# An index load moved to SyncE's queue, and VectorE's work around the first expert in another order

## Chip, core and metric

The kernel runs on one core of a Trainium2 chip. The metric is the device time of one execution in microseconds, the median of several runs. TensorE (PE in the profile) multiplies, VectorE (DVE) and ScalarE (ACT) work element by element, GpSimd (POOL) issues the indirect transfers, and SyncE (SP) issues the other transfers from one queue in program order.

## What is computed

```python
attn_out = _attn_ref(q, k, v, lam)          # decayed linear attention, (4, 8, 768, 64)
x = attn_out.transpose(0, 2, 1, 3).reshape(3072, 512)
logits = x @ w_gate                          # 8 experts
e_idx = np.argmax(logits, axis=1)
gate_w = probs[np.arange(N), e_idx]          # softmax of the logits
eom = 1.0 / (1.0 + np.exp(-(x @ w_output_gate)))
for e in range(E):
    mask = e_idx == e
    h = np.maximum(x[mask] @ w1[e], 0.0)     # 512 -> 1024
    ye = h @ w2[e]                           # 1024 -> 512
    out[mask] = gate_w[mask, None] * eom[mask, e, None] * ye
```

Every token goes to one of eight experts, so the tokens must be sorted by expert before the second half.

## The kernel before

**First half.** The attention runs over 24 tiles of 128 tokens (6 chunks by 4 batches). Each finished tile is transposed by VectorE (`stage_d2`) and written to a table of rows in memory, `x_d`. After every four tiles the router ranks their tokens (`route_choose`, `route_place`), and `place_scatter` lets GpSimd scatter one record a token (its output row, its scale, its row of `x_d`) into a table `tab_d`, which is ordered by expert and place.

**Second half.** The experts are worked off from the fullest to the emptiest. For each, the index rows are read back out of `tab_d` (`load_rows`), turned into row numbers on VectorE (`row_index`, which writes `rows`), the tokens' rows are fetched from `x_d` by GpSimd (`gather`), transposed (`x_turn`), and split into a high and a low float32r part (`x_split`). The weights come in pieces of 1 MB (`load_piece` on SyncE, into one of three `raw` buffers) and are split the same way: ScalarE makes the high part (`split_hi`, L132, `whi`), VectorE the low part (`split_lo2`, L146, `wlo`). Each product is three matmuls: high by high, low by high, high by low (L85, L86, L87).

**The first expert.** It starts before the last four tiles are routed. Its 448 rows come in three parts. The first 192 are gathered early. The middle rows, below place `LATE` = 352, are read once the first five groups of tiles are scattered: `load_rows(0, 1, 3, nc.gpsimd)` reads their index from GpSimd's own queue. The last 96 are picked from the last four tiles on TensorE (`take_late`, the tile `chosen`) and split by `split_late`. `units` is the list of TensorE's work on the first 192 rows: eight columns `fc` of the up product (tiles `ph`, 12 matmuls each), then two blocks of the down product (`pyr`, 24 matmuls each; the first block reads pieces 2 and 3, that is `w2`). `fill(n)` takes n units from it, and `settle()` makes the activations of those that are done: `hhi` on ScalarE (L1009) and `hlo` on VectorE (L1010). After the down blocks TensorE goes on with the up product for rows 192 to 447.

**What sets the order.** Inside `manual_schedule` every engine runs its instructions in the order in which the code writes them. Semaphores hold an instruction until its inputs are there, and everything behind it on that engine or queue then waits too. The stretch that the change touches stands between the last attention tile and the loop over the experts:

```python
place_scatter(B)                       # the last tiles' records
settle()
for h in range(2):
    split_lo2(1, h)
...
row_index(0, 1)
gather(0, 6, 11, LAST * P)
stage_d2(LAST + 1)
stage_d2(n - 1, 2)
split_late()
sort_rest(counts)
...
    fill(8)
    split_lo2(2, h)
    settle()
```

Of the kernel before, what the change touches and what calls it, by code (L numbers as in the profile page):

```python
# [23 lines left out]
def kernel(  # L24
# [96 lines left out]
    def split_hi(i, j):  # L121
        if i >= len(pieces):
            return
        if pieces[i] not in wparts:
            wparts[pieces[i]] = (
                wpool.tile([P, 4, 512], F32R, tag="whi", bufs=4, name=f"whi_{i}"),
                wpool.tile([P, 4, 512], F32R, tag="wlo", bufs=4, name=f"wlo_{i}"),
            )
        src, hi = raws[i][:, j, :], wparts[pieces[i]][0][:, j, :]
        if turned_out(i):  # L130
            src, hi = by_quarter(src), by_part(hi)
        nc.scalar.copy(out=hi, in_=src)  # L132
# [163 lines left out]
    def blank_rows():  # L296
        norow = wpool.tile([P, E * EB * 3], I32, tag="raw", bufs=3, name="norow")
        nc.gpsimd.memset(norow, NOROW)
        nc.sync.dma_start(tab_d.rearrange("(p r) t -> p (r t)", p=P), norow)


    later = []
# [220 lines left out]
    def stage_d2(n, count=1):  # L523
        if count == 1:
            xn = slot(f"xn_{n}")
        else:
            xn = pool.tile([P, 8 * P], F32, tag="wide", bufs=4, name=f"xn_{n}")
        for i in range(count):

            src = live[n + i]["xT"].rearrange("p (g b r) -> p b g r", g=NPAIR, b=4)  # L530
            dst = xn[:, i * DM : (i + 1) * DM].rearrange("p (b g c) -> p b g c", b=4, g=NPAIR)
            nc.vector.transpose(dst, src)
            weave()
        nc.sync.dma_start(
            x_d[n * P : (n + count) * P, :].rearrange("(i p) m -> p i m", p=P),
            xn[:, 0 : count * DM].rearrange("p (i m) -> p i m", m=DM),
        )
# [133 lines left out]

    pending = []

    def place_scatter(count):
        for _ in range(min(count, len(pending))):
            idx, rec = pending.pop(0)
            scatter(
                "table",
                nc.gpsimd.indirect_dma_start(  # L679
                    out=tab_d,  # L680
                    out_offset=bass.IndirectOffsetOnAxis(ap=idx, axis=0),
                    in_=rec,
                    in_offset=None,
                    bounds_check=P * E * EB - 1,
                    oob_is_err=False,
                ),
            )

    def scatter(group, ins):
        inst = getattr(ins, "ins", ins)  # L690
        tc.declare_no_dep(inst, group=group, reason="these scatters write different rows")
        tc.add_to_no_dep_group(group, inst)
# [135 lines left out]
    def load_rows(p, j0=0, j1=None, eng=nc.sync):  # L828
        if p >= E:
            return  # L830
        n = (KT[p] if j1 is None else j1) - j0
        t = const.tile([32, 4, n, 3], I32, name=f"index_{p}_{j0}")
        src = tab_v[bass.ds(expert[p], 1)][:, :, j0 : j0 + n, :]
        eng.dma_start(t, src.rearrange("e (b r) j t -> (e r) b (j t)", b=4))
        idxs[(p, j0)] = (t, n)

    def load_outs(p, j0=0, j1=None):
        if p >= E:
# [25 lines left out]
    def row_index(p, j0=0):  # L864
        if p >= E:
            return
        t, n = idxs[(p, j0)]
        gf = const.tile([32, 4, n], F32, name=f"rowf_{p}_{j0}")
        nc.vector.scalar_tensor_tensor(
            out=gf, in0=t[:, :, :, 2], scalar=float(4 * NT), in1=t[:, :, :, 2], op0=ALU.is_lt, op1=ALU.mult  # L870
        )
        gi = const.tile([P, 4, n], I32, name=f"rows_{p}_{j0}")
        for qq in range(4):
            nc.vector.tensor_scalar(
                out=gi[32 * qq : 32 * qq + 32], in0=gf, scalar1=float(P * qq), scalar2=None, op0=ALU.add
            )
        for j in range(n):
            for bb in range(4):
                gis[(p, 4 * (j0 + j) + bb)] = gi[:, bb, j : j + 1]
# [326 lines left out]
    def settle():  # L1206
        while acts:
            acts.pop(0)()
# [8 lines left out]
    with tc.manual_schedule():  # L1217
# [126 lines left out]
        for f in held[6:]:  # L1344
            f()
        place_scatter(B)
        load_rows(0, 1, 3, nc.gpsimd)
        stage_c(n - 1)
        for g in range(NPAIR):
            x_hi(0, g, 0)  # L1350
# [30 lines left out]
        fill(4)  # L1381
        take_late(LAST)
        at_once(place[4:])
        place_scatter(B)
        settle()
        for h in range(2):
            split_lo2(1, h)
        for j in range(4):
            split_hi(2, j)
        row_index(0, 1)  # L1390
        gather(0, 6, 11, LAST * P)
        stage_d2(LAST + 1)
        stage_d2(n - 1, 2)
        split_late()
        sort_rest(counts)
        expert_regs(1, order_i[:, 1:2], 1)
        load_rows(1)
        load_piece(4)
        load_outs0()
        expert_regs(2, order_i[:, 2:E], E - 2)  # L1400
        for h in range(2):
            split_hi(3, 2 * h)
            split_hi(3, 2 * h + 1)
            fill(8)
            split_lo2(2, h)
            settle()
        for h in range(2):
            split_lo2(3, h)
            fill(2)
        row_index(1)  # L1410
        gather(1, 0, 4)
        settle()
# [199 lines left out]
```

## Time and profile before

| | us |
|---|---|
| median of 3 runs | 416.05 |
| lowest and highest | 414.84, 416.11 |
| the profiled execution: its time | 415.14 |
| its span, first to last instruction | 413.4 |
| TensorE busy in the span | 400.8 (97%) |
| VectorE, ScalarE, GpSimd busy | 286.7, 190.4, 238.8 |
| mean granted TensorE clock | 0.998 |

The profiled execution's time is its span and 1.74 us around it. Times in the rows further down count from the span's start. TensorE is busy nearly all the time, so a change pays only where TensorE waits.

### The profile page before, as it was taken

The page shows a single profiled execution, that of the slowest core. Times are in us where ns is not written, and L with a number is a line of the kernel's source. Part 1 is how long each engine was busy: PE and PEld are TensorE (multiplying, and loading weights), DVE is VectorE, ACT ScalarE, POOL GpSimd, SP SyncE. Part 2 cuts the span into 40 slices and gives each one's busy share as a digit, 9 for nine tenths or more (in the row PEclk, how much of TensorE's full clock was granted, in tenths as well). Part 3 has the DMA queues.
Part 4 walks back from the last instruction along what each step waited for, and adds up shares of the span by engine and source line. Part 5 has one row for each costly group of instructions (what it writes and reads, how often), then busy time and mean ns, then how long its engine had stood idle before and what let it go on. Part 6 is the DMA issues. An engine that isn't in the chain of part 4 may idle for free.

```text
span 413.4 us, 10570 instructions
## 1 busy us (share of the span) xinstructions
PE 400.8 (97%) x3869; PEld 367.1 (89%) x3869; DVE 286.7 (69%) x810; ACT 190.4 (46%) x460; POOL 238.8 (58%) x301
## 2 busy tenths in 40 slices
PE   7999999999899999999999999999999999999994
PEld 4889878798698698999999999999999989989983
DVE  2759697877888646876868857957965864873710
ACT  4767665665684033544145325504704543542400
POOL 5367679668846788674783665467386266120012
PEclk9999999999999999999999999999999999999999
DMA  8999898889972764544479548746846884461001
GB/s 177 231 254 246 226 258 224 215 230 259 322 231 79 222 206 144 170 141 135 150 209 297 198 135 241 262 178 200 292 140 186 295 271 151 127 224 46 5 27 52
DMA packets 95103, 79.11 MB, mean 191 GB/s; under 512 B 58445, under 2 KB 70769, under 8 KB 95041
## 3 DMA queue, kind: packets, MB, share of 16 engines
q1 hardware_dynamic: 88080, 64.88, 53.2%
q0 software_dynamic: 6240, 12.93, 10.0%
q8 instruction: 32, 0.52, 0.5%
q10 hardware_dynamic: 720, 0.53, 0.5%
q14 instruction: 31, 0.25, 0.2%
HBM read 62.25 MB, written 16.45 MB: 190 GB/s over the span
## 4 chain that ended last, share of the span: by engine, by line
PE 85%; DVE 6%; DMA 5%; issue 2%; POOL 1%; ACT 0%; POOLq 0%; DVEq 0%; SPq 0%
PE ph_None L86 10%; PE ph_None L87 10%; PE ph_None L85 10%; PE py L87 6%; PE py L86 6%; PE py L85 6%; PE pyr L86 5%; PE pyr L87 5%; PE pyr L85 5%; PE ps L400 4%; PE po L441 4%; PE pk L341 3%; PE po L424 2%; PE pq L341 2%; DVE at L409 2%; PE pst L454 2%
## 5 line engine op out<-in xcount | busy, mean ns | idle before, releaser
L900 POOL DMA_INDIRECT xg<-x_d,rows x100 | 110.6, 1106 | 54.8 <-issue 28.9
L1009 ACT ACTIVATE hhi<-ph_None 128x400 fp32r<-128x400 f32 (+4 forms) x56 | 28.1, 501 | 115.8 <-PE ph_None L87 111.0
L86 PE MATMUL ph_None<-xlo,whi 128*128 128x400 f32 (+4 forms) x224 | 76.2, 340 | 0.0
L87 PE MATMUL ph_None<-xhi,wlo 128*128 128x400 f32 (+4 forms) x224 | 76.1, 340 | 0.0
L85 PE MATMUL ph_None<-xhi,whi 128*128 128x400 f32 (+4 forms) x224 | 76.1, 340 | 0.0
L132 ACT CAST whi<-raw 128x512 fp32r<-128x512 f32 x128 | 74.7, 615 | 2.4 <-DMA raw<-in_moe_w_dram 2.4
L141 DVE TENSOR_TENSOR wlo<-raw,whi 128x512 fp32r<-128x512 f32 x112 | 74.5, 686 | 0.7 <-ACT whi L132 0.5
L1010 DVE SCALAR_TENSOR_TENSOR hlo<-ph_None,hhi 128x400 fp32r<-128x400 f32 (+4 forms) x56 | 31.9, 570 | 35.2 <-ACT hhi L1009 33.2
L87 PE MATMUL py<-hhi,wlo 128*128 128x400 f32 (+2 forms) x128 | 44.4, 347 | 0.0
L86 PE MATMUL py<-hlo,whi 128*128 128x400 f32 (+2 forms) x128 | 44.4, 347 | 0.0
L85 PE MATMUL py<-hhi,whi 128*128 128x400 f32 (+2 forms) x128 | 44.4, 347 | 0.0
L86 PEld LDWEIGHTS ph_None<-xlo,whi 128*128 128x128 f32 x224 | 42.0, 188 | 0.5 <-DVE xlo L935 0.2
L1126 POOL DMA_INDIRECT out_dram<-yn,table x12 | 12.5, 1045 | 51.8 <-DVE yn L1190 34.6
L85 PEld LDWEIGHTS ph_None<-xhi,whi 128*128 128x128 f32 x224 | 42.0, 188 | 0.4
L87 PEld LDWEIGHTS ph_None<-xhi,wlo 128*128 128x128 f32 x224 | 42.0, 188 | 0.2
L345 ACT COPY qT<-pq 64x256 f32<-64x256 f32 x96 | 37.8, 393 | 2.0 <-PE pq L341 1.0
L409 DVE TENSOR_TENSOR at<-ps,decay 128x512 f32<-128x512 f32 x48 | 31.1, 681 | 10.4 <-PE ps L400 10.4
L86 PE MATMUL pyr<-wlo,hhi 128*128 128x512 f32 (+2 forms) x96 | 37.8, 394 | 0.5 <-DVE wlo L146 0.5
L87 PE MATMUL pyr<-whi,hlo 128*128 128x512 f32 (+2 forms) x96 | 37.6, 391 | 0.0
L85 PE MATMUL pyr<-whi,hhi 128*128 128x512 f32 (+2 forms) x96 | 37.5, 390 | 0.0
L931 ACT CAST xhi<-y 128x256 fp32r<-128x256 f32 (+3 forms) x64 | 19.5, 357 | 31.5 <-DVE y L917 31.5
L679 POOL DMA_INDIRECT tab_d<-rec,idx x24 | 26.2, 1090 | 10.0 <-issue 4.1
(216 smaller groups left out, 783.0 us busy)
## 6 DMA issues: line engine op xcount, KB each, us to landing
raw<-in_moe_w_dram SPq DMA_DIRECT2D x32, 1024.0 KB
x_d<-xn SPq DMA_DIRECT2D x22, 256.0 KB
qkv<-in_k_dram SPq DMA_DIRECT2D x40, 128.0 KB
qkv<-in_v_dram SPq DMA_DIRECT2D x20, 256.0 KB
qkv<-in_q_dram SPq DMA_DIRECT2D x36, 128.0 KB
yd<-yo SPq DMA_DIRECT2D x12, 256.0 KB
yr<-yd SPq DMA_DIRECT2D x48, 64.0 KB
xg<-x_d,rows POOLq DMA_INDIRECT x100
```

The lines of the kernel that those rows point to most:

```text
L85: nc.tensor.matmul(ps, a[0], b[0], start=first, stop=False)
L86: nc.tensor.matmul(ps, a[0], b[1], start=False, stop=False)
L87: nc.tensor.matmul(ps, a[1], b[0], start=False, stop=last)
L132: nc.scalar.copy(out=hi, in_=src)
L141: eng.tensor_tensor(out=lo, in0=src, in1=hi.bitcast(F32), op=ALU.subtract)
L341: nc.tensor.transpose(out=dst[:, m * P : (m + 1) * P], in_=src[:, m], identity=ident)
L345: copies = [lambda r=r, view=view, src=src: nc.scalar.copy(out=view(qT[r]), in_=src) for r, view, src in query_parts(pq)]
L409: nc.vector.tensor_tensor(out=at, in0=ps.rearrange("p (g t) -> p g t", g=NPAIR), in1=dec[:, j], op=ALU.mult)
L679: nc.gpsimd.indirect_dma_start(out=tab_d, out_offset=bass.IndirectOffsetOnAxis(ap=idx, axis=0), in_=rec, in_offset=None, bounds_check=P * ...
L900: nc.gpsimd.indirect_dma_start(out=xg[(p, i)][:, m * P : (m + 1) * P], out_offset=None, in_=x_q[0 : 4 * rows], in_offset=bass.IndirectOffs ...
L1009: nc.scalar.activation(out=hi[:, r], in_=ph[:, r], func=AF.Relu)
L1010: nc.vector.scalar_tensor_tensor(out=lo[:, r], in0=ph[:, r], scalar=0.0, in1=hi[:, r].bitcast(F32), op0=ALU.max, op1=ALU.subtract,)
```

## The change

The index load of the first expert's middle rows moves from GpSimd's queue to SyncE's. It becomes two transfers of 12 bytes a row, which read only places below `LATE`, into a tile that is preset to "no row" early in the program. The last tiles' scatters, which write places from `LATE` on, are declared independent of it. `split_lo2(2, 0)` and `sort_rest` move ahead of `row_index(0, 1)`, `split_lo2(2, 1)` moves behind the `settle()` of its turn, `stage_d2` of the last three tiles and `split_late` move behind the low parts of piece 3, and `load_piece(4)` moves ahead of `load_rows(1)`.

```diff
@@ blank_rows
         nc.sync.dma_start(tab_d.rearrange("(p r) t -> p (r t)", p=P), norow)
+        nc.gpsimd.memset(middle_t, NOROW)
@@ place_scatter
-    def place_scatter(count):
+    def place_scatter(count, beside=()):
...
+            scatter("table", ins)
+            for other in beside:
+                tc.declare_no_dep(
+                    getattr(ins, "ins", ins), other,
+                    reason="the first expert's places below LATE are read, the last tiles' places begin at LATE",
+                )
@@ new
+    middle_t = const.tile([32, 4, 2, 3], I32, name="index_0_1")
+
+    def load_middle():
+        parts = []
+        idxs[(0, 1)] = (middle_t, 2)
+        for j in range(2):
+            nb = min(4, (LATE - P * (j + 1)) // 32)
+            src = tab_v[bass.ds(expert[0], 1)][:, 0 : 32 * nb, 1 + j : 2 + j, :]
+            ins = nc.sync.dma_start(middle_t[:, 0:nb, j, :], src.rearrange("e (b r) j t -> (e r) b (j t)", b=nb))
+            parts.append(getattr(ins, "ins", ins))
+        return parts
@@ after the loop over the tiles
         place_scatter(B)
-        load_rows(0, 1, 3, nc.gpsimd)
+        middle = load_middle()
         stage_c(n - 1)
@@ the last tiles
-        place_scatter(B)
+        place_scatter(B, middle)
         settle()
         for h in range(2):
             split_lo2(1, h)
         for j in range(4):
             split_hi(2, j)
+        split_lo2(2, 0)
+        sort_rest(counts)
         row_index(0, 1)
         gather(0, 6, 11, LAST * P)
-        stage_d2(LAST + 1)
-        stage_d2(n - 1, 2)
-        split_late()
-        sort_rest(counts)
         expert_regs(1, order_i[:, 1:2], 1)
+        load_piece(4)
         load_rows(1)
-        load_piece(4)
         load_outs0()
         expert_regs(2, order_i[:, 2:E], E - 2)
         for h in range(2):
             split_hi(3, 2 * h)
             split_hi(3, 2 * h + 1)
             fill(8)
-            split_lo2(2, h)
             settle()
+            if h == 0:
+                split_lo2(2, 1)
         for h in range(2):
             split_lo2(3, h)
             fill(2)
+        stage_d2(LAST + 1)
+        stage_d2(n - 1, 2)
+        split_late()
         row_index(1)
         gather(1, 0, 4)
```

TensorE's own order stays as it is. Three engines' orders decide what reaches it when.

VectorE, from the low parts of piece 1 (`wlo_2663`) to the last low part of the up product (`hlo_7`), before the change. `wlo_2810` is the low part of piece 2, `xn` are the transposed tiles, `keys` opens `sort_rest`, and `rowf_1` opens `row_index(0, 1)`:

```order
L146 TENSOR_TENSOR wlo_2663<-raw_2299,whi_2662 128x1024 x2
L869 SCALAR_TENSOR_TENSOR rowf_1_2815<-index_1_2566 32x8
L874 TENSOR_SCALAR rows_1_2817<-rowf_1_2815 32x8 x4
L532 STREAM_TRANSPOSE xn_2839<-xT_2493 128x512
L980 TENSOR_TENSOR xlo_0_2580<-chosen,xhi_0_2579 128x96
L732 SCALAR_TENSOR_TENSOR keys<-pcount,eidx 128x8
L146 TENSOR_TENSOR wlo_2810<-raw_2411,whi_2809 128x1024
L1010 SCALAR_TENSOR_TENSOR hlo_3_2965<-ph_3_0_2937,hhi_3_2964 128x192
L146 TENSOR_TENSOR wlo_2934<-raw_2597,whi_2933 128x1024 x2
L869 SCALAR_TENSOR_TENSOR rowf_0_3024<-index_0_2870 32x16
L1010 SCALAR_TENSOR_TENSOR hlo_7_3045<-ph_7_0_3010,hhi_7_3044 128x192
```

The same stretch of VectorE after the change (`wlo_2665` is piece 1's low part, `wlo_2812` piece 2's, `wlo_2922` piece 3's):

```order
L146 TENSOR_TENSOR wlo_2665<-raw_2301,whi_2664 128x1024 x2
L146 TENSOR_TENSOR wlo_2812<-raw_2413,whi_2811 128x1024
L736 SCALAR_TENSOR_TENSOR keys<-pcount,eidx 128x8
L885 SCALAR_TENSOR_TENSOR rowf_1_2824<-index_1_157 32x8
L890 TENSOR_SCALAR rows_1_2826<-rowf_1_2824 32x8 x4
L1026 SCALAR_TENSOR_TENSOR hlo_3_2952<-ph_3_0_2925,hhi_3_2951 128x192
L146 TENSOR_TENSOR wlo_2922<-raw_2599,whi_2921 128x1024 x2
L533 STREAM_TRANSPOSE xn_3011<-xT_2495 128x512
L996 TENSOR_TENSOR xlo_0_2582<-chosen,xhi_0_2581 128x96
L885 SCALAR_TENSOR_TENSOR rowf_0_3026<-index_0_2860 32x16
L1026 SCALAR_TENSOR_TENSOR hlo_7_3047<-ph_7_0_2997,hhi_7_3046 128x192
```

The transposes and the late rows' low parts went from ahead of the weights' low parts to behind them; the same instructions stand between the first and the last row of both.

SyncE's queue around the load of piece 3 (`raw_2597`), before the change. `xn_2475` is the first of the last four tiles, and `raw_2872` is piece 4:

```order
L534 DMA x_d<-xn_2475 128x512
L119 DMA raw_2597<-in_moe_w_dram 128x4x512
L534 DMA x_d<-xn_2839 128x512
L534 DMA x_d<-xn_2842 128x2x512
L738 TENSOR_LOAD order_i
L834 DMA index_0_2870<-tab_d 32x4x12
L119 DMA raw_2872<-in_moe_w_dram 128x4x512
```

The same place of the queue after the change; piece 3 is `raw_2599`, piece 4 `raw_2858`, and `index_1_157` is the tile of the middle rows' index:

```order
L535 DMA x_d<-xn_2477 128x512
L849 DMA index_1_157<-tab_d 32x4x3
L849 DMA index_1_157<-tab_d 32x3x3
L119 DMA raw_2599<-in_moe_w_dram 128x4x512
L742 TENSOR_LOAD order_i
L119 DMA raw_2858<-in_moe_w_dram 128x4x512
L838 DMA index_0_2860<-tab_d 32x4x12
L535 DMA x_d<-xn_3011 128x512
```

Two reads of `tab_d` now stand between the last early row write and piece 3, and the last tiles' rows are written after the next expert's index load.

ScalarE from piece 2's high parts (`whi_2811`) on, after the change; before it, the four casts of `chosen` stood between the first two of these rows:

```order
L132 CAST whi_2811<-raw_2413 128x512 x4
L132 CAST whi_2921<-raw_2599 128x512 x2
L1025 ACTIVATE hhi_3_2951<-ph_3_0_2925 128x192
L1025 ACTIVATE hhi_4_2955<-ph_4_0_2938 128x192
L132 CAST whi_2921<-raw_2599 128x512 x2
L1025 ACTIVATE hhi_5_2988<-ph_5_0_2962 128x192
L1025 ACTIVATE hhi_6_2992<-ph_6_0_2975 128x192
L993 CAST xhi_0_2581<-chosen 128x96
L1025 ACTIVATE hhi_7_3046<-ph_7_0_2997 128x192
```

Piece 3's high parts (`whi_2921`) still stand ahead of the activations `hhi_3` to `hhi_7`.

## Rows read from the trace of the kernel before

**Rows 1.** The page, part 1: busy us, share of the span, instructions.

```profile
PE 400.8 (97%) x3869; PEld 367.1 (89%) x3869; DVE 286.7 (69%) x810; ACT 190.4 (46%) x460; POOL 238.8 (58%) x301
```

**Rows 2.** Windows: length, busy PE, PEld, DVE, ACT, POOL, clock, DMA share, GB/s.

```profile
131.50:138.70 7.20, 6.70 (x27) 4.31 (x27) 6.65 (x14) 0.33 (x1) 5.84 (x5) 1.00 0.45 140
...
138.60:407.50 268.90, 268.85 (x1465) 254.70 (x1463) 180.27 (x462) 105.09 (x236) 143.28 (x162) 1.00 0.55 177
```

**Rows 3.** Waits of PE's weight loads from 116 us on: total, times, longest.

```profile
PEld pyr L86 <- DVE wlo L146: 1.7, 3, 0.8
PEld pyr L87 <- DVE hlo L1010: 0.4, 1, 0.4
```

**Rows 4.** Timeline of PE: start, duration, instruction, idle time before and releaser.

```profile
131.52 0.41 PE L85 MATMUL pyr<-whi,hhi 128*128 128x512 f32 x1
132.43 0.50 PE L86 MATMUL pyr<-wlo,hhi 128*128 128x512 f32 x1 [0.49 <-DVE wlo L146]
...
138.31 0.50 PE L87 MATMUL pyr<-whi,hlo 128*128 128x512 f32 x1
138.65 0.40 PE L85 MATMUL pyr<-whi,hhi 128*64 128x512 f32 x1
...
144.18 0.28 PE L85 MATMUL ph<-xhi,whi 128*128 128x256 f32 x1
```

**Rows 5.** Timeline of DVE, 123 to 142 us.

```profile
123.50 2.35 DVE L146 TENSOR_TENSOR wlo<-raw,whi 128x1024 fp32r<-128x1024 f32 x2
126.82 0.16 DVE L869 SCALAR_TENSOR_TENSOR rowf<-index 32x8 f32<-32x8 int32 x1 [0.97 <-DMA index<-tab_d]
...
127.73 1.90 DVE L532 STREAM_TRANSPOSE xn<-xT 128x512 f32<-128x512 f32 x3
...
130.19 0.15 DVE L732 SCALAR_TENSOR_TENSOR keys<-pcount,eidx 128x8 f32<-128x8 f32 x1
...
131.15 1.22 DVE L146 TENSOR_TENSOR wlo<-raw,whi 128x1024 fp32r<-128x1024 f32 x1
...
137.90 0.36 DVE L1010 SCALAR_TENSOR_TENSOR hlo<-ph,hhi 128x192 fp32r<-128x192 f32 x1
141.74 0.91 DVE L917 STREAM_TRANSPOSE y<-xg 128x512 f32<-128x512 f32 x2 [3.48 <-DMA xg<-x_d,rows]
```

**Rows 6.** Timeline of ACT, 125 to 127 us.

```profile
125.54 1.17 ACT L132 CAST whi<-raw 128x512 fp32r<-128x512 f32 x2
126.58 0.36 ACT L1009 ACTIVATE hhi<-ph 128x192 fp32r<-128x192 f32 x1
```

**Rows 7.** Timeline of SP: start and duration of the issue, not of the transfer.

```profile
116.69 0.38 SPq L119 DMA_DIRECT2D raw<-in_moe_w_dram  x1
...
134.41 0.36 SPq L834 DMA_DIRECT2D index<-tab_d  x1
135.02 0.39 SPq L119 DMA_DIRECT2D raw<-in_moe_w_dram  x1
```

**Rows 8.** What SP's queue waited for, 95 to 172 us.

```profile
SPq L834 <- DMA tab_d<-rec,idx: 1.6, 1, 1.6
```

**Rows 9.** Timeline of POOL, 30 to 140 us.

```profile
31.00 0.18 POOL L862 CAST beat<-oh 1x1 f32<-1x1 bf16 x1 [2.94 <-DVE oh L584]
...
119.08 0.97 POOL L679 DMA_INDIRECT tab_d<-rec,idx  x1 [0.30 <-issue]
124.14 0.63 POOL L834 DMA_DIRECT2D index<-tab_d  x1 [4.10 <-DMA tab_d<-rec,idx]
...
131.63 1.59 POOL L679 DMA_INDIRECT tab_d<-rec,idx  x1 [0.30 <-issue]
...
140.80 0.99 POOL L900 DMA_INDIRECT xg<-x_d,rows  x1 [0.30 <-DMA xg<-x_d,rows]
```

**Rows 10.** DMA view, 134 to 142 us: busy tenths in 40 slices of 0.2 us; GpSimd's queue: packets, MB.

```profile
DMA  0000000364882278999999999999959100009299
...
q0 software_dynamic: 160, 0.33, 14.0%
```

More of the change, by code (lines that the diff above doesn't have):

```diff
@@ L672 @@
     pending = []
-    def place_scatter(count):
+    def place_scatter(count, beside=()):
         for _ in range(min(count, len(pending))):
             idx, rec = pending.pop(0)
[L677 to L686, printed above, removed]
-            )
+            ins = nc.gpsimd.indirect_dma_start(
+                out=tab_d,
+                out_offset=bass.IndirectOffsetOnAxis(ap=idx, axis=0),
+                in_=rec,
+                in_offset=None,
+                bounds_check=P * E * EB - 1,
+                oob_is_err=False,
+            )
+            scatter("table", ins)
[4 more added lines that the diff above has]
+                )
     def scatter(group, ins):
```

## The prediction

> **What bounds the kernel now.** I read the page's engine shares first: TensorE is busy 400.8 of 413.4 us [rows 1]. The windows then say where the rest lies. From 138.6 us to its last matmul TensorE is busy 268.85 of 268.90 us [rows 2], so whatever the change does before 138.6 us passes to the end unless it makes a new wait behind it. The window just ahead, 131.5 to 138.7 us, is the one with a hole. It is the first down block of the first expert, 24 matmuls: its first starts at 131.52 and the next block's first at 138.65, 7.13 us. The second block has the same 24 matmuls and takes from 138.65 to 144.18, 5.53 us [rows 4]. So 1.60 us of waiting stand in the first block. The list of waits names what ended them: three waits of weight loads for `wlo` and one for `hlo` [rows 3]. In the timeline the first is the 0.49 us at 132.43, and the last is the matmul at 138.31, the third one of column 7, which starts right behind `hlo_7`, done at 137.90 + 0.36 = 138.26 [rows 4, 5].
>
> All four releasers stand on VectorE, so its timeline is read next. From 123.50 to 138.26 it has one real pause, 0.97 us at 126.82, where `row_index(0, 1)` waits for the index that GpSimd's queue loads [rows 5]. Everything else is work back to back. So in this stretch VectorE is the bound, and TensorE's last wait ends when VectorE has finished a fixed list of instructions.
>
> **The change, part by part.**
>
> *VectorE's list.* The orders show that the change moves instructions between the low part of piece 1 and `hlo_7`, but the same ones stand between these two before and after. Putting the weights' low parts first removes TensorE's first three waits, yet the fourth stays: `hlo_7` still comes behind the transposes, the late rows and `row_index(1)`. The time won at the first three is waited again at the fourth. What counts is when VectorE reaches the end, that is, its pauses. The old pause of 0.97 us goes if the index is there in time. That is all that this list can give: at most -0.97 us, not 1.60.
>
> *The index.* Its load must wait until the earlier scatters have landed. The last is issued at 119.08 and takes 0.97 us; GpSimd waited until 124.14 for it [rows 9]. In that time the transfer of piece 3, issued at 116.69 [rows 7], was under way, and after the change it is not. A later scatter, with less beside it, started at 131.63, ended at 133.22, and SyncE's index load, which waited 1.6 us for it, was issued at 134.41, 1.19 us after that end [rows 7, 8, 9]. So SyncE is released at 119.08 + 0.97 + 1.19 = 121.2, or at 121.9 if counted from the scatter's start (134.41 - 131.63 = 2.78); I take 121.4. The upper bound is 124.1, as before. GpSimd's load of 124.14 was awaited until 126.82 [rows 5, 9], 2.7 us; the two on SyncE, issued 0.61 us apart, are there by 124.7 (by 127.4 at the late bound). VectorE asks for them at 123.50 + 2.35 = 125.85, plus 1.17 for one more `wlo` (half of that 2.35), plus 0.96 for `sort_rest` (130.19 to 131.15), at 127.98 [rows 5]. No wait at either bound: the 0.97 us are gone.
>
> *What is queued behind the index load.* This is the price. On SyncE the load of piece 3 now follows the two index loads, where before it was issued at 116.69 [rows 7]. SyncE's index load and the load behind it are issued 134.41 and 135.02, 0.61 us apart, so piece 3 is issued at 121.4 + 2 x 0.61 = 122.6, 5.9 us later than before. The transfer: piece 4, issued at 135.02, keeps the DMA engines busy until about 140.3, the last busy slices of that window [rows 7, 10], 5.3 us, with 0.33 MB of GpSimd's transfers in the same window. Piece 3 would have only 12-byte scatters beside it, so I take 5.0 us (bounds 4.5, when 0.33 of 1.38 MB is taken off the 3.4 us of full slices, and 5.4) and have it landed at 127.6. The DMA engines do not make up for the late issue: the Trainium skill, "DMA: Bandwidth & Descriptors", section "Anatomy of one DMA", says that a semaphore is waited for on the issuing sequencer before dispatch, and SyncE's wait of 1.6 us with piece 4's issue right behind agrees [rows 7, 8].
>
> Who waits for piece 3: ScalarE's casts of it, and behind them in its order `hhi_3` and the later activations. From the casts' start to the end of the first activation it took 126.58 + 0.36 - 125.54 = 1.40 us [rows 6]. So `hhi_3` is done at 127.6 + 1.40 = 129.0. VectorE reaches `hlo_3` at 127.98 + 0.91 for `row_index(0, 1)` (126.82 to 127.73) = 128.89 [rows 5]. It waits 0.11 us. Later activations are made faster (two casts and two activations against two `hlo` and a `wlo` of 1.22 us) and cost nothing more.
>
> *The sum.* -0.97 + 0.11 = -0.86 us; each microsecond by which piece 3 lands later than 127.5 takes one back.
>
> The same page and section give a fit for one transfer, 2.0 us plus bytes over 436 GB/s. By that estimate 1 MB takes 4.4 us, piece 3 lands at 127.0, no wait is left, and the sum is -0.97; the trace's own row of a quiet load is slower, so I stay with rows.
>
> *Edits that I cost at nothing.* The preset of the tile: one small GpSimd instruction early, ahead of an idle of 2.94 us at 31.00 [rows 9]; without that cover some 0.2 us (the row's own length). The scatters of the last tiles no longer wait for the index, so they start near 123 instead of 127.7, and the gathers behind them follow `rows` at 128.9 rather than a table that is complete at 134. Before, VectorE waited 3.48 us for these rows at 141.74 while TensorE was in the second block; the second block ends 0.9 us earlier at 143.3, and the rows come some 3 us earlier, so that cover holds. The last tiles' rows of `x_d` are written after 136 instead of from 128.5 on. GpSimd's first gather for the next expert needs them: transposes end about 1.8 us before `hlo_7` at 137.4, and with some 3 us to land the gather goes at 138.6, still ahead of its 140.80 of before [rows 9]. `load_piece(4)` comes some 5 us earlier than 135.02 and costs nothing.
>
> **The rivals.**
>
> *All four waits vanish.* -1.60 us, 414.5. For it: each has a releaser that the new order brings forward. Against: the order of VectorE, where `hlo_7` is still the last. It needs VectorE's list to be shorter than the sum of its rows, by 0.6 us at least.
>
> *It changes nothing.* Piece 3 lands at 128.5, the new pause is as long as the old: 0.0, 416.05. That takes 0.9 us more than I count, half of it in the release and half in the transfer. For it: the piece that I take the transfer from showed 5.3, not 5.0.
>
> *Slower: piece 3 is held.* If the scatters land as late as before, SyncE is released at 124.1, piece 3 is issued at 125.3 and lands at 130.4 with 5.1 us. `hhi_3` is done at 131.8, VectorE waits 2.9 us, and the sum is +1.9 us, 418.0. It decides from a landing at 128.5 on, and shows from 129.8. For it: the only row of these very scatters says 124.14. Against: that row has piece 3 itself in the way, which the change removes.
>
> **How the numbers follow.** The profiled execution took 415.14 us, its span 413.4 and 1.74 around it; the forecast for it is 414.3. It lies 0.91 us below the median of the three runs, so set against the median the same change gives 416.05 - 0.86 = 415.2. The runs shown lie within 1.27 us, about 0.3%, which is also what a measurement of this kernel can tell from no change. Chances: forecast 0.55, all four waits 0.17, nothing 0.15, slower 0.13. The forecast and "nothing" are both inside 0.3% (1.25 us), with a few in a hundred that fall beyond by the runs' own spread; the four waits are outside. Faster 0.21, same 0.66, slower 0.13. The range reaches from 0.3 below the four waits' 414.5, for the runs' spread, to a landing of piece 3 at about 129.3 with its +0.8: 414.2 to 416.9. The likeliest case's own range is 414.9 to 415.8.
>
> **What would show it.** In the profile after: no wait of DVE's `rowf` at `row_index(0, 1)`; SyncE's two index issues near 121.4 and piece 3's near 122.6; ACT idle from about 124 to 127.6 for `raw`; a DVE wait of some 0.1 us at `hlo_3`; no PE wait for `wlo`, but one of about 0.6 us for `hlo_7` (the block's last matmul would start at 131.52 + 23/24 x 5.53 = 136.8, and `hlo_7` is done at 137.4); the second block at about 137.8 instead of 138.65; then dense TensorE to the end. Wrong would be: piece 3 later than 128.5, a DVE wait for the next expert's index ahead of `hlo_7`, or a wait of TensorE behind 144 us for rows of `x_d`.

## The result, and the profile after

The changed kernel took 421.63 us, the median of six runs (420.54 to 423.62), where the kernel before took 415.88 beside it. The ratio is 1.0116, with a 95% interval of 1.0082 to 1.0149: slower by 1.2 per cent. The forecast was 415.2, and 416.9 at most.

The profiled execution after took 423.62 us, the longest of its six, and its span is 422.0 us, 8.6 more than before. Three marks on TensorE split that. The first matmul of `pcount`, the last routing step ahead of the experts, starts at 122.54 us (118.23 before): 4.31. From there to the first down block both kernels need 13.3 us. From that block to the first matmul of the second expert (`ph_None`) it takes 38.85 us (135.82 to 174.67) where it took 35.12 (131.52 to 166.64): 3.73. The rest, to the end, is 247.35 against 246.80: 0.55. The first part turns out to be no work of the change (experiments, below); the second is what the change did.

The marks of the kernel before that [rows 4] does not show:

```profile
118.23 0.18 PE L728 MATMUL pcount<-cum,ones 128*128 128x8 bf16 x1
...
166.64 0.36 PE L85 MATMUL ph_None<-xhi,whi 128*128 128x432 f32 x1
```

The timeline of TensorE after, in that stretch (start, duration, instruction, idle time before it and what ended it):

```profile
122.54 0.18 PE L732 MATMUL pcount<-cum,ones 128*128 128x8 bf16 x1
...
135.82 0.42 PE L85 MATMUL pyr<-whi,hhi 128*128 128x512 f32 x1
...
142.26 0.50 PE L87 MATMUL pyr<-whi,hlo 128*128 128x512 f32 x1 [1.00 <-DVE hlo L1026]
142.59 0.39 PE L85 MATMUL pyr<-whi,hhi 128*64 128x512 f32 x1
...
148.11 0.28 PE L85 MATMUL ph<-xhi,whi 128*128 128x256 f32 x1
...
165.02 0.51 PE L87 MATMUL pyr<-whi,hlo 128*128 128x512 f32 x1 [0.67 <-DVE hlo L1026]
165.73 0.50 PE L85 MATMUL pyr<-whi,hhi 128*128 128x512 f32 x1 [0.21 <-ACT hhi L1025]
...
174.67 0.47 PE L85 MATMUL ph_None<-xhi,whi 128*128 128x432 f32 x1 [2.10 <-ACT xhi L947]
```

The first down block is shorter, 6.77 us for 7.13. The three waits for `wlo` are gone, and one of 1.00 us for `hlo_7` is left. The loss comes later, at 165 to 175 us; in the same stretch the kernel before had no wait of TensorE. The windows (columns as in [rows 2]) put its size beside it:

```profile
135.80:142.60 6.80, 5.80 (x27) 4.43 (x27) 6.34 (x16) 0.33 (x1) 4.64 (x5) 1.00 0.50 160
...
160.00:176.00 16.00, 12.87 (x54) 9.44 (x53) 8.73 (x23) 4.88 (x14) 12.37 (x17) 1.00 0.39 114
176.00:416.00 240.00, 240.00 (x1292) 230.17 (x1290) 163.55 (x422) 95.10 (x209) 118.76 (x134) 1.00 0.55 177
```

Between 160 and 176 us TensorE is idle for 3.13 us at full clock; from 176 us on it is dense. From the second block's end to `ph_None` it takes 26.56 us (148.11 to 174.67) where it took 22.46 (144.18 to 166.64), 4.10 more; what is above 3.13 shows as no idle time in these rows. All those waits end with VectorE or ScalarE, so VectorE's timeline is next:

```profile
132.31 0.15 DVE L885 SCALAR_TENSOR_TENSOR rowf<-index 32x8 f32<-32x8 int32 x1
...
133.44 0.62 DVE L1026 SCALAR_TENSOR_TENSOR hlo<-ph,hhi 128x192 fp32r<-128x192 f32 x2
...
137.91 1.89 DVE L533 STREAM_TRANSPOSE xn<-xT 128x512 f32<-128x512 f32 x3
...
140.79 0.17 DVE L885 SCALAR_TENSOR_TENSOR rowf<-index 32x16 f32<-32x16 int32 x1 [0.35 <-DMA index<-tab_d]
...
141.84 0.36 DVE L1026 SCALAR_TENSOR_TENSOR hlo<-ph,hhi 128x192 fp32r<-128x192 f32 x1
...
163.94 0.71 DVE L933 STREAM_TRANSPOSE y<-xg 128x512 f32<-128x512 f32 x1 [4.76 <-DMA xg<-x_d,rows]
...
173.03 1.20 DVE L933 STREAM_TRANSPOSE y<-xg 128x512 f32<-128x512 f32 x2 [2.76 <-DMA xg<-x_d,rows]
```

The old pause at the first expert's `rowf` is gone, as forecast. At 163.94 and 173.03 VectorE waits 4.76 and 2.76 us for the rows of the second expert. The kernel before had two waits at the same places:

```profile
155.79 0.71 DVE L917 STREAM_TRANSPOSE y<-xg 128x512 f32<-128x512 f32 x1 [0.53 <-DMA xg<-x_d,rows]
...
164.90 1.14 DVE L917 STREAM_TRANSPOSE y<-xg 128x512 f32<-128x512 f32 x2 [2.78 <-DMA xg<-x_d,rows]
```

So only the first wait is longer, by 4.23 us. The second is as long as it was, but what it waits for comes later: its transpose starts 37.21 us behind the first down block's start, where it was 33.38. The rows are gathered by GpSimd, whose timeline has one hole, beside [rows 9]:

```profile
122.63 0.97 POOL L678 DMA_INDIRECT tab_d<-rec,idx  x1 [0.30 <-issue]
...
133.71 0.97 POOL L678 DMA_INDIRECT tab_d<-rec,idx  x1 [0.30 <-issue]
...
140.66 1.00 POOL L916 DMA_INDIRECT xg<-x_d,rows  x1 [0.31 <-issue]
149.28 1.00 POOL L916 DMA_INDIRECT xg<-x_d,rows  x1 [7.62 <-DVE yn L1206]
...
173.10 1.00 POOL L916 DMA_INDIRECT xg<-x_d,rows  x1 [0.30 <-issue]
```

The first gather of the second expert goes at 149.28 us, 13.45 us behind the first down block's start (worked out before rounding). Before it was 140.80, 9.28 us behind that start. From this gather to the one at 173.10 GpSimd never idles for more than 0.31 us, and neither did it before from 140.80 to 164.95, so a first gather that is 4.2 us later makes all the later rows late. The label "DVE yn" is not its releaser: the gather reads `x_d`, and the last rows of `x_d` land at 148.5 in the trace's records. Why so late, SyncE's timeline shows (beside [rows 7]; a row stands for the issue) and the waits of its queue (total, times, longest) beside [rows 8]:

```profile
124.79 0.91 SPq L849 DMA_DIRECT2D index<-tab_d  x2
126.27 0.40 SPq L119 DMA_DIRECT2D raw<-in_moe_w_dram  x1
...
133.27 0.39 SPq L119 DMA_DIRECT2D raw<-in_moe_w_dram  x1
138.73 0.33 SPq L838 DMA_DIRECT2D index<-tab_d  x1
139.25 1.83 SPq L868 DMA_DIRECT2D table<-tab_d  x3
144.04 0.82 SPq L535 DMA_DIRECT2D x_d<-xn  x2
145.13 0.39 SPq L119 DMA_DIRECT2D raw<-in_moe_w_dram  x1
```

```profile
SPq L838 <- DMA tab_d<-rec,idx: 4.9, 1, 4.9
```

VectorE was done with the last transposes at 137.91 + 1.89 = 139.80. The `x_d` writes were issued 4.24 us after that. Ahead of them on SyncE stand the second expert's index load, which waited 4.9 us for the last scatter, three table loads until 141.08, and then 2.96 us in which SyncE reads six experts' numbers into registers (`expert_regs(2)`). The load of the six registers itself takes 1.27 us in the trace, and the other 1.7 us are register operations behind it. The Trainium skill, "Runtime: NRT & Kernel Launch", section "Instruction fetch mechanics", puts a register load at about 0.2 us a register; the page's loads come from device memory, and this one reads a tile on the core. By that figure six would take 1.2 us, as an estimate, close to the 1.27; the figure leaves the other 1.7 out.

### The profile page after: what moved, and what is told of

It is laid out like the page before. It is cut to its first block, busy times and chain, and to the rows that moved or that the text cites. A ratio compares the mean times of both kernels' runs of the same rounds, so it can differ in the third digit from the quotient of the medians.

```text
span 422.0 us, 10570 instructions
## 1 busy us (share of the span) xinstructions
PE 401.9 (95%) x3869; PEld 367.9 (87%) x3869; DVE 287.4 (68%) x810; ACT 190.4 (45%) x460; POOL 236.3 (56%) x301
## 4 chain that ended last, share of the span: by engine, by line
PE 73%; DMA 8%; DVE 7%; POOL 5%; issue 4%; SPq 1%; ACT 1%; POOLq 0%; DVEq 0%
PE ph_None L85 10%; PE ph_None L86 10%; PE ph_None L87 9%; PE py L87 6%; PE py L86 6%; PE py L85 6%; DMA xg<-x_d,rows 4%; PE pyr L86 3%; PE pyr L85 3%; PE pyr L87 3%; PE ps L401 3%; POOL xg L916 3%; PE po L442 3%; DVE at L410 2%; DMA qkv<-in_q_dram 2%
## 5 line engine op out<-in xcount | busy, mean ns | idle before, releaser
L916 POOL DMA_INDIRECT xg<-x_d,rows x100 | 108.6, 1086 | 65.7 <-issue 32.7
L678 POOL DMA_INDIRECT tab_d<-rec,idx x24 | 27.4, 1141 | 13.8 <-issue 9.4
```

Source lines behind the costliest of these rows:

```text
L678: ins = nc.gpsimd.indirect_dma_start(out=tab_d, out_offset=bass.IndirectOffsetOnAxis(ap=idx, axis=0), in_=rec, in_offset=None, bounds_chec ...
L916: nc.gpsimd.indirect_dma_start(out=xg[(p, i)][:, m * P : (m + 1) * P], out_offset=None, in_=x_q[0 : 4 * rows], in_offset=bass.IndirectOffs ...
```

## The experiments

Each kernel was timed beside the kernel before on the same chip. The four series ran on chips of different pace (the kernel before took 425.2, 426.4, 416.9 and 426.8 us in them), so times are compared within a series only. On the slower chips the profiles have stalls of all engines with no releaser ("issue") between about 135 and 170 us; no stage length is read from those. What is read is where an instruction stands against the first down block's start. This table has it from all profiles: when SyncE (in `xd_act` ScalarE) issues the first of the two late `x_d` writes, and when GpSimd issues the second expert's first gather.

| kernel | `x_d` write, us behind the block's start | gather | ratio to before (95%) |
|---|---|---|---|
| before | -3.05 | 9.28 | 1 |
| after | 8.22 | 13.45 | 1.0116 (1.0082 to 1.0149) |
| after_again | 8.50 | 13.24 | 1.0122 (1.0082 to 1.0162) |
| after_third | 8.83 | 13.58 | 1.0109 (1.0061 to 1.0157) |
| reorder_only | 9.37 | 14.01 | 1.0094 (1.0059 to 1.0128) |
| issue_only | 8.03 | 13.39 | 1.0085 (1.0051 to 1.0119) |
| piece4_behind | 8.07 | 12.90 | 1.0123 (1.0077 to 1.0168) |
| piece4_behind_2 | 7.34 | 12.14 | 1.0091 (1.0057 to 1.0124) |
| tables_behind | 3.83 | 9.12 | 1.0030 (0.9991 to 1.0069) |
| tables_behind_2 | 4.27 | 9.03 | 0.9989 (0.9960 to 1.0018) |
| queue_clean | 3.68 | 9.30 | 0.9982 (0.9949 to 1.0015) |
| xd_act | 4.79 | 9.13 | 1.0048 (1.0008 to 1.0088) |
| xd_early | -0.79 | 9.57 | 1.0005 (0.9960 to 1.0050) |
| both_back | -0.78 | 7.22 | 0.9983 (0.9954 to 1.0012) |
| middle_only | -2.95 | 7.92 | 1.0000 (0.9963 to 1.0038) |
| preset_only | -3.74 | 7.25 | 1.0040 (0.9994 to 1.0086) |
| settle_first | -1.64 | 6.54 | 0.9971 (0.9936 to 1.0006) |
| before_settle | -4.11 | 8.20 | 0.9975 (0.9937 to 1.0013) |

In the table, every kernel whose gather goes by 9.6 us is level with the kernel before, `xd_act` with its 1.0048 apart, and every kernel whose gather goes at 12.1 us or later is slower by 0.85 to 1.23 per cent. Where the write goes 3.6 us or more behind the block's start, the gather follows it by 4.3 to 5.6 us. `after_again` and `after_third` repeat the loss in two more series, so it is not the spread of one.

The theories: A, the loss is the late place of the `x_d` writes in SyncE's queue. B, it is the index load on SyncE and the piece 3 that it delays. C, part of it lies in the first half, set off by the preset.

**Halves of the change.** `preset_only` is the kernel before with the preset.

```diff
         nc.sync.dma_start(tab_d.rearrange("(p r) t -> p (r t)", p=P), norow)
+        nc.gpsimd.memset(middle_t, NOROW)
```

> The kernel before with the early preset of the index tile alone. Theory A (the loss stands on SyncE's queue behind 122 us): no difference, 415.9 us within 0.5, pcount's first matmul at about 118.2 us. Rival C (part of the loss is in the first half, set off by the preset): pcount's matmul 1.8 to 4.3 us later and the time at 417.7 to 420.

The interval reaches from no change to 0.9 per cent, so the time alone does not rule out C. What does is `middle_only` and `both_back`, which hold the same preset and show no loss, and `reorder_only`, which has no preset and shows it. The late `pcount` of the profile after is not the change's either: `before_settle` and `issue_only` run the code of before up to that point and start `pcount` at 120.71 and 121.20 us, and `settle_first`, which runs the changed code up to there, starts it at 118.91.

`middle_only` is the kernel before with the index load on SyncE, and what it needs:

```diff
-        load_rows(0, 1, 3, nc.gpsimd)
+        middle = load_middle()
...
-        place_scatter(B)
+        place_scatter(B, middle)
```

> The kernel before with only the index load moved to SyncE (and what it needs: preset, scatters not behind it); the low parts, the x_d writes and piece 4 stay where they were. Theory A: x_d writes stay early and piece 4 stays behind the index load, so nothing of the loss is here, 415.2 to 416.2 us. Rival B: piece 3 is late by about 5.9 us and held, the time 417.5 to 420. Rival C (the preset): 417.7 or more.

No change in time, so B falls. Piece 3 did come late here (issued 126.16 us) and ScalarE waited for it:

```profile
131.34 1.14 ACT L132 CAST whi<-raw 128x512 fp32r<-128x512 f32 x2 [1.96 <-DMA raw<-in_moe_w_dram]
```

`reorder_only` is the changed kernel with that half undone, the preset too:

```diff
-        middle = load_middle()
+        load_rows(0, 1, 3, nc.gpsimd)
...
-        place_scatter(B, middle)
+        place_scatter(B)
```

> The other half of the change alone: the index load on GpSimd's queue as before and piece 3 early, but low parts, x_d writes and piece 4 in the changed order. Theory A: the loss is here as in the changed kernel, ratio to before 1.008 to 1.015, x_d writes behind the tables and register reads. Rival B: no loss, 0.996 to 1.002.

The loss is here. So it sits in the order, not in the index load.

**The place of the `x_d` writes.** `issue_only` changes nothing in the kernel before but the place of two instructions on SyncE. `stage_d2` puts its write into a list, which is worked off later:

```diff
-        stage_d2(LAST + 1)
-        stage_d2(n - 1, 2)
+        hold = []
+        stage_d2(LAST + 1, 1, hold)
+        stage_d2(n - 1, 2, hold)
...
         expert_regs(2, order_i[:, 2:E], E - 2)
+        for write in hold:
+            write()
```

> The kernel before with one thing changed: the two x_d writes of the last tiles are issued by SyncE behind the register reads for the other experts (the transposes on VectorE stay early, the index load stays on GpSimd, piece 4 stays behind the next index load). Theory A: the writes go some 9 to 10 us behind the first down block's start instead of 2 to 3 us ahead of it, the second expert's first gather 13 us or more behind that start, and the ratio to before is 1.006 to 1.012. If the late transposes on VectorE or the whole changed order were the cause, and not the place in SyncE's queue: 0.997 to 1.003.

That alone costs 0.85 per cent. The timelines of SyncE, GpSimd, VectorE and TensorE and two windows, in this order, repeat the picture of the changed kernel, with transposes done at 131.53:

```profile
137.69 1.85 SPq L858 DMA_DIRECT2D table<-tab_d  x3
142.51 0.83 SPq L535 DMA_DIRECT2D x_d<-xn  x2
```

```profile
147.87 0.99 POOL L906 DMA_INDIRECT xg<-x_d,rows  x1 [5.34 <-PE ph L87]
```

```profile
162.24 0.71 DVE L923 STREAM_TRANSPOSE y<-xg 128x512 f32<-128x512 f32 x1 [4.96 <-DMA xg<-x_d,rows]
...
171.35 1.14 DVE L923 STREAM_TRANSPOSE y<-xg 128x512 f32<-128x512 f32 x2 [2.79 <-DMA xg<-x_d,rows]
```

```profile
172.93 0.47 PE L85 MATMUL ph_None<-xhi,whi 128*128 128x432 f32 x1 [0.46 <-ACT xhi L937]
```

```profile
160.00:165.00 5.00, 3.75 (x15) 2.26 (x13) 2.77 (x7) 2.02 (x7) 4.52 (x7) 1.00 0.17 52
165.00:170.00 5.00, 5.00 (x15) 3.98 (x16) 3.46 (x10) 1.13 (x3) 4.30 (x7) 0.66 0.71 228
```

TensorE loses 1.25 us in one window, and in the next its granted clock is 0.66, between its two levels of 1.2 and 2.4 GHz. The matmuls at half speed are not paid on top of the waits here. From the first down block to `ph_None` it takes 38.45 us (134.48 to 172.93), where the changed kernel, at full clock from 160 us on, took 38.85. The wait ahead of `ph_None` is 0.46 us instead of 2.10. By these two profiles the slow matmuls run in time in which TensorE would have waited for the second expert's rows; no run sets the clock by itself.

**What stands ahead of them.** `tables_behind` moves the table loads and register reads behind the writes:

```diff
-        load_outs0()
-        expert_regs(2, order_i[:, 2:E], E - 2)
...
         stage_d2(LAST + 1)
         stage_d2(n - 1, 2)
+        load_outs0()
+        expert_regs(2, order_i[:, 2:E], E - 2)
         split_late()
```

> The changed kernel, with the three table loads, the load of the order and its register reads moved behind the x_d writes of the last tiles on SyncE. Theory A: the x_d writes are issued at about 140 instead of 144.0 us, the first gather for the second expert goes at about 145 instead of 149.3, the waits of TensorE at 165 to 175 us shrink from about 4.6 to about 1 us, and the time falls from 421.6 to about 418. Rival B (the late piece 3 and the index load on SyncE are the loss): no difference, 421.6 within 0.6. Rival C: no difference either.

`piece4_behind` only puts piece 4 back:

```diff
-        load_piece(4)
         load_rows(1)
+        load_piece(4)
```

> The changed kernel with load_piece(4) back behind load_rows(1). Theory A in its narrow form (piece 4 in the way of the last scatter, so SyncE's wait for it is 4.9 us): that wait falls to about 1.6 us, the x_d writes and the second expert's gathers come 3 us earlier, about 2 to 3 us of the loss go, ratio to before 1.004 to 1.007. If what stands behind the index load on SyncE (tables, register reads) is what matters and not piece 4: the x_d writes move by under 1 us and the ratio stays near 1.012.

In its first profile SyncE's register reads lasted longer than in the changed kernel (4.20 us for 2.96; that profile has stalls in this stretch, which may be part of it), so both were run once more in one series, with the changed kernel (`after_third`, which repeats `after_again`) and with `queue_clean`, which does both moves:

> The changed kernel once more, beside the runs of the kernel before on this chip, where the kernel before itself may take longer than 416. If the loss belongs to the change: ratio to before near 1.012, x_d writes issued some 8 us behind pcount's first matmul plus 13, that is 21 to 22 us behind it, and the first gather of the second expert 26 to 27 us behind it (before: 10.2 and 22.6). If the loss was the spread of one series of runs (rival D): ratio 1.000 within 0.004, with the same late x_d writes.

> The changed kernel as the anchor of this series: ratio to before near 1.012 as in the two series so far, the second expert's first gather some 13 us behind the first down block's start.

> Piece 4 back behind the next index load, x_d writes still behind the tables and register reads; once more, since SyncE's register reads lasted 2.8 instead of 1.6 us in the first profile. If piece 4 in the way of the last scatter carries the loss: gather about 10.5 us behind the first down block's start, ratio 1.003 to 1.006. If the tables and register reads carry it: gather 11.5 or more behind it, ratio 1.008 to 1.013.

> Tables and register reads moved behind the x_d writes, piece 4 still ahead of the index load. If the tables and register reads carry the loss: gather about 9 us behind the first down block's start, ratio 1.000 to 1.004. If piece 4 carries it: ratio 1.008 or more.

```diff
-        load_piece(4)
         load_rows(1)
-        load_outs0()
-        expert_regs(2, order_i[:, 2:E], E - 2)
...
         stage_d2(LAST + 1)
         stage_d2(n - 1, 2)
+        load_piece(4)
+        load_outs0()
+        expert_regs(2, order_i[:, 2:E], E - 2)
         split_late()
```

> Only the next index load stands ahead of the late x_d writes on SyncE; piece 4, the tables and the register reads stand behind them. VectorE's transposes are as late as in the changed kernel. If the late transposes by themselves cost nothing: x_d writes within 0.5 us of the transposes' end, gather 7.5 to 9 us behind the first down block's start, ratio 0.997 to 1.001. If they cost: 1.004 or more.

The tables and register reads carry the loss: with them behind the writes none is measured (1.0030 and 0.9989, both intervals include 1), with piece 4 alone put back it is still there (1.0123 and 1.0091, changed kernel 1.0122 and 1.0109 in the same series). Two things stay unparted. The register reads lasted 4.09 us in the second profile of `piece4_behind` too, so SyncE gave back there part of what the shorter wait for the scatter had won. And no run moves the tables (1.83 us of the queue in the profile after) and the register reads (2.96 us) one at a time. VectorE's late transposes by themselves cost nothing: in `queue_clean` they end 4.84 us behind the block's start, and SyncE's writes and GpSimd's gather follow them at once, with waits that name their true releasers:

```profile
138.55 0.32 SPq L838 DMA_DIRECT2D index<-tab_d  x1
141.34 1.57 SPq L535 DMA_DIRECT2D x_d<-xn  x2
```

```profile
146.95 1.00 POOL L916 DMA_INDIRECT xg<-x_d,rows  x1 [2.59 <-DMA x_d<-xn]
```

The windows of `after_third`, and behind them one of `queue_clean`, are no measure of the loss. TensorE's idle time in them has no releaser in its timeline; these are the stalls named above. They show that the granted clock falls behind some of these stalls (0.52) and not behind others: in `queue_clean` it is 1.00 in this window and in those from 160 to 176 us.

```profile
160.00:165.00 5.00, 1.91 (x11) 1.49 (x11) 1.12 (x2) 0.89 (x2) 4.52 (x8) 1.00 0.27 66
165.00:170.00 5.00, 4.22 (x11) 2.77 (x11) 1.66 (x3) 0.89 (x2) 3.40 (x6) 0.52 0.15 39
```

```profile
155.00:160.00 5.00, 2.72 (x15) 1.89 (x14) 0.43 (x1) 0.39 (x1) 3.03 (x4) 1.00 0.87 265
```

**Other ways round the queue.** `xd_act` is the changed kernel with the two writes issued from ScalarE's queue:

```diff
-        stage_d2(LAST + 1)
-        stage_d2(n - 1, 2)
+        stage_d2(LAST + 1, 1, nc.scalar)
+        stage_d2(n - 1, 2, nc.scalar)
```

> The changed kernel with only the two late x_d writes issued from ScalarE's queue, so that they wait for the transposes alone. Theory A: they go as soon as the transposes are done (about 4 us behind the first down block's start, 4 us sooner than in the changed kernel), the second expert's first gather about 9 us behind that start, ratio to before 0.998 to 1.004, about 0.9 per cent under the changed kernel. If the late transposes are the cause: still 1.008 or more.

It stands 0.7 per cent under the changed kernel (ratios of two series, whose intervals just touch), less than forecast. The gather comes as early as in `tables_behind`. The likely rest is a new wait: ScalarE now stands behind the transposes, and in the one profile, of this kernel's longest execution, TensorE waits for its activations.

```profile
143.94 0.50 PE L85 MATMUL pyr<-whi,hhi 128*128 128x512 f32 x1 [1.64 <-ACT hhi L1025]
145.69 0.80 PE L87 MATMUL pyr<-whi,hlo 128*128 128x512 f32 x1 [1.02 <-DVE hlo L1026]
```

`xd_early` puts transposes, writes and late rows back, with piece 4 still ahead of the index load. `both_back` puts piece 4 back too.

```diff
         gather(0, 6, 11, LAST * P)
+        stage_d2(LAST + 1)
+        stage_d2(n - 1, 2)
+        split_late()
...
-        stage_d2(LAST + 1)
-        stage_d2(n - 1, 2)
-        split_late()
```

> The changed kernel, with the last tiles' transposes, their x_d writes and the late rows back at the place they had before, ahead of the next expert's index load. Theory A: x_d writes issued near 131 us, the first gather of the second expert follows the index rows at about 142 to 143 us, no waits of TensorE behind 150 us, the time 416 to 417.5. Rival B: still 420 or more. Rival C: 418.5 to 420, since only the later half of the loss goes.

> The changed kernel with piece 4 behind the index load and the last tiles' transposes, x_d writes and late rows ahead of it, as before; the index load on SyncE and the low parts' order stay changed. Theory A: everything late on SyncE is undone, no wait of VectorE for the second expert's index or rows, ratio to before 0.996 to 1.001. Rival B (piece 3 late and the index load on SyncE cost): 1.006 or more.

Both are level with the kernel before. In the profile of `xd_early`, an execution longer than most, VectorE waits for the index load that stands behind piece 4, ahead of `hlo_7`; the profile of `both_back` has no such wait. The times do not tell the two apart.

```profile
143.79 0.17 DVE L885 SCALAR_TENSOR_TENSOR rowf<-index 32x16 f32<-32x16 int32 x1 [2.48 <-DMA index<-tab_d]
```

**The list on VectorE.** `settle_first` is `both_back`, and `before_settle` the kernel before, with `hlo_7` ahead of the next expert's row numbers:

```diff
-        row_index(1)
-        gather(1, 0, 4)
         settle()
+        row_index(1)
+        gather(1, 0, 4)
```

> The version with piece 4 and the x_d writes back at their old places, index load and low parts as changed, and in addition the last hlo of the first half ahead of the second expert's row index on VectorE. By my step on VectorE's list (its end ends the last wait of TensorE in the first down block) the last wait there shrinks by the 1.05 us of the row index, and the ratio to before is 0.994 to 0.998. If that wait is not the bound: the same as without it, 0.998.

> The kernel before with only the last hlo of the first half ahead of the second expert's row index on VectorE. By my step on VectorE's list: TensorE's last wait in the first down block falls by its whole 0.4 to 0.6 us, ratio 0.998 to 0.999, too small to be told by the time, so the block's length in the profile decides (7.13 us before, 6.5 to 6.7 by this step, 7.1 if the list does not bound it).

Both medians are lower than before's (415.38 and 416.50 against 416.93), but both intervals include 1, so no version is shown to beat the kernel before. The first down block took 6.18 us in `settle_first` and, in `before_settle`, from 133.99 to the next row's start:

```profile
133.99 0.41 PE L85 MATMUL pyr<-whi,hhi 128*128 128x512 f32 x1
...
139.79 0.40 PE L85 MATMUL pyr<-whi,hhi 128*64 128x512 f32 x1
```

That is 5.80 us for 7.13. Only part of it is the move: in `issue_only`, where VectorE's order is that of before, the block took 6.20 us (134.48 to 140.68). The pause of 0.97 us at the index [rows 5] is in neither profile.

## Why the prediction was wrong

- **The step that failed** is in "Edits that I cost at nothing": "GpSimd's first gather for the next expert needs them: transposes end about 1.8 us before `hlo_7` at 137.4, and with some 3 us to land the gather goes at 138.6". The transposes were on time: forecast 135.6, 4.1 us behind the block's start of 131.52, measured 139.80 - 135.82 = 3.98. The gather was not: forecast 7.1 us behind that start, measured 13.45. I let the write follow the transposes, and did not count what stands ahead of it on SyncE in its new place: of the 6.4 us, 4.24 are the write's wait in SyncE's queue. (Counted by the rows, the 1.8 us lead to `hlo_7`'s start and not to its end at 137.4, so that the transposes would end near 135.3; the step does not hang on it.) The prediction's last sign of error, a wait of TensorE behind 144 us for rows of `x_d`, is what the profile shows. `issue_only` shows what this place costs by itself: 0.85 per cent (0.51 to 1.19), 3.5 us of that series' 416.93.
- **The landing** was mis-sized as well. From the first write's issue to the gather it took 149.28 - 144.04 = 5.24 us; I had 3. Of that the second write, from 144.49 on, took 4.0 us, with piece 5 issued at 145.13 right behind it. By itself this costs nothing: in `queue_clean` the gather follows the write by 5.6 us, and no loss is measured.
- **"`load_piece(4)` comes some 5 us earlier than 135.02 and costs nothing"** was wrong in the profile. It was issued just ahead of the last scatter (133.27 and 133.71), and SyncE's wait for that scatter grew from 1.6 [rows 8] to 4.9 us. With piece 4 put back, SyncE's index load goes 1.17 us after the scatter's end in `piece4_behind`, where it went 4.05 us after it. In the times it is small: 1.0123 and 1.0091 without it, 1.0122 and 1.0109 with it, which these intervals do not tell apart.
- **The gain** had the right sign and was mis-sized: -0.86 forecast, 7.13 to 6.77 = -0.36 measured in the block. I had named a wait for the next expert's index ahead of `hlo_7` as a sign of error, and it is there, 0.35 us at 140.79. The pause that the gain rests on is not in every execution: the profiles of `issue_only`, `before_settle` and `preset_only`, with GpSimd's load of before, do not have it. In `issue_only`, where VectorE's order is that of before too, the block took 6.20 us, less than the 6.77 after. So the 0.36 us compares with one execution that had the pause, and no run shows it as a gain.
- **Right in mechanism and size:** SyncE was released 1.19 us after the last scatter's end (122.63 + 0.97 = 123.60, issue 124.79). The three waits for `wlo` went and the one for `hlo_7` stayed. Piece 3 took 5.2 us from its issue to the casts (126.27 to 131.47) where I had 5.0, and cost VectorE nothing at `hlo_3` (133.44, no idle). The 4.4 us that I quoted beside it come from the Trainium skill's fit for transfers that GpSimd issues ("DMA: Bandwidth & Descriptors", section "Anatomy of one DMA"), and SyncE issued this one; the measured 5.2 decides.
- **The rivals.** The slower one, piece 3 held, was not what happened: the time ended on its side, and beyond its 418.0, by another mechanism, and `middle_only` shows that a late piece 3 costs nothing measurable.
- **Open:** the changed kernel's 1.2 per cent against `issue_only`'s 0.85 (their intervals overlap), and why the profiled execution came by its 4.31 us ahead of `pcount`. Kernels with the old code there vary by up to 3 us too. The trace shows where part of it lies: a matmul at 115.67 waits 1.06 us for VectorE, and from 116 to 118 us the granted clock is 0.50, where the profile before has 1.00. `issue_only`, with the old code in this stretch, has 0.51 from 114 to 116 us.

## What to carry to other kernels

When an instruction that issues a transfer is moved, write down everything between its old and its new place on the issuing queue, with the waits and the register reads, and find the latest reader of what it moves; the time at which its input is ready is only a lower bound. A write that feeds the next stage belongs ahead of loads for later stages in a queue that runs in program order. An earlier load can lengthen a wait if a small transfer that others wait for is issued just behind it; here it lengthened SyncE's, and the times do not show what that cost.

## What the runs showed of the hardware

- Idle time of TensorE was followed by a lower granted clock in some executions: windows with 0.66 (`issue_only`) and 0.52 (`after_third`) behind windows in which it was busy 3.75 and 1.91 of 5 us. In others it was not: `queue_clean` was busy 2.72 of 5 us and stayed at 1.00. In the profiled run of the changed kernel the clock was 0.50 from 116 to 118 us, behind a wait of 1.06 us, and 1.00 through the 3.13 us of waiting between 160 and 176 us.
- GpSimd's scatters took 2.05 us at 127.89 and 1.90 at 130.24, each begun beside one of VectorE's `wlo` subtractions of 127.80 to 131.28, and 0.97 us at 132.44 behind them. The Trainium skill, "SBUF — State Buffer", section "SBUF: two separate sides", says that VectorE with two operands in this memory and a GpSimd operation that reads from it lock each other out, whichever starts first. These rows agree, and so does the scatter at 119.09, which took 1.96 us and began during the subtractions of 117.86 to 120.21.
- The 12-byte records of the last scatter, issued 0.44 us behind piece 4's 1 MB on another queue, let SyncE go 138.73 - 134.68 = 4.05 us after the scatter's end, where the quiet one took 1.19 and the last scatter of `piece4_behind`, with piece 4 behind it, 1.17.
